# Top-k attention with a highway layer on one core: one exponential for a pair of items, and GpSimd in the search for the 32nd score

## Chip, core and metric

The kernel runs on one NeuronCore of a Trainium2 chip. The metric is device time in microseconds of one execution; before the change the median of three runs is 806.49 us (806.15 to 808.53).

## What is computed

Attention over 8 batches and 8 heads with 576 rows of 64 columns, in which each row of scores keeps its 32 largest, followed by a highway layer of 512 columns. Inputs q, k and v are normal draws times 0.1.

```python
scores = scale * np.matmul(q, k.transpose(0, 1, 3, 2))
kth = np.partition(scores, -top_k, axis=-1)[..., -top_k:-top_k + 1]   # top_k = 32
scores = np.where(scores >= kth, scores, -1000000000.0)
scores = scores - np.max(scores, axis=-1, keepdims=True)
attn = np.exp(scores)
attn = attn / (np.sum(attn, axis=-1, keepdims=True) + 1e-09)
x = np.matmul(attn, v)            # heads side by side: 4608 rows of 512
H = np.maximum(x @ w_h, 0.0)
T = 1.0 / (1.0 + np.exp(-(x @ w_t + b_t)))
out = T * H + (1.0 - T) * x
```

## The kernel before, in words

**Items and pairs.** An item is a tile of 128 score rows by 576 columns. For each batch and each of four full query tiles (`qt` 0 to 3) there is one item per head; the last 64 rows of two heads together form one "remainder" item. That makes 36 items and 18 pairs a batch (16 of full tiles, 2 of remainders), 144 pairs in all (`NG`). `step(i)` (L775) is called once per pair, and its order is written out by hand; each engine works through its own instructions in the order in which the calls issue them. One call holds parts of several pairs: masks of pair i, segment maxima of pair i+1, scores of pair i+2, masking of pair i-1, and the attention output of pair i-3.

**The search for the 32nd score** of a row goes so.
- `scores` (L296) puts both items' scores into one of two PSUM buffers (`xps`); TensorE may start on pair i+2 when pair i's buffer has had its last reader, the second `below`.
- `copy_scores` (L346) copies both items' scores from PSUM to SBUF in one ScalarE instruction of 1152 columns (`sc`).
- `segments` (L351) takes the 8 largest of each of six segments of 96 columns, 12 instructions a pair on VectorE.
- `refine` (L358) makes from them, in a handful of small VectorE instructions (`high`, `low`, `neg`, L373 to L382), the row's maximum (column `TOP` of `wall`) and a threshold (`THR`), which is surely among the 24th to 32nd score.
- `mask_count` (L395) on ScalarE marks the scores at or above the threshold and counts them by the accumulator (`csum`). `mask_add` (L407) adds that mark on TensorE to the scores in PSUM, so that `below` (L419) on VectorE finds the eight largest scores under the threshold.
- The threshold and these eight are nine candidates. `hits` (L423, VectorE) writes a 1 where the count says that the candidate is the 32nd; `pick_a` (L434, GpSimd) multiplies these flags by the candidates; `pick_b` (L438, VectorE) sums, which gives the 32nd score (`KTH`, `kth(u)`).

**What is made of it.** `biases` (L390) on GpSimd prepares for a pair the two biases of its exponentials (minus scale times each item's maximum) and of the Relu of the pair before it (`be`, one instruction of four columns; it is made to wait for the second masking of that step by `after`, L474, and `above_one` of GpSimd stands behind it). `expo` (L414) on ScalarE computes the exponential of one item, 576 columns, with its own bias: in a step the first item's stands before the copy of the next pair's scores and the second's behind it, behind the scores of pair i+2 (L819, L836). The masking of the pair follows one step later: item 0 by a Relu on ScalarE that is large from the 32nd on (`above`, L441) and a minimum on VectorE (`keep_min`, L447); item 1 by a comparison on GpSimd (`above_one`, L452) and a product on VectorE (`keep_mul`, L457), or, where GpSimd has other work, by one longer VectorE instruction (`keep`, L462).

**The rest.** A DMA transposes each masked item (L481); three steps later `values` (L487) multiplies it by V. V carries an extra column of ones (L138), so that the sum of the weights comes out beside the output. `xs_copy` (L507) takes four heads' outputs from PSUM to SBUF on ScalarE; after the eighth head of a tile, `back_xs` (L755) hands the block of 128 rows to `ffn_pieces` (L549), which divides by the sums (L557: sum plus 1e-9, times 2) and runs the highway layer in pieces: elementwise parts on GpSimd (`do_work`, L683), matmuls on TensorE, Relu and Tanh on ScalarE. `spare` (L274) issues filler matmuls that write to the same PSUM tile as the outputs, so they wait for `xs_copy` where that has the tile.

**The end.** `finish` (L943) does the last two pairs and blocks in an order of its own. Three checks (`sure`, L932, ScalarE, each a Sign with an accumulated count) test that the search was sound in all rows; only if one fails does the program compute everything again by a slow way (L1048 on).

Of the kernel before, what the change touches and what calls it, by code (L numbers as in the profile page):

```python
# [26 lines left out]
def kernel(  # L27
# [10 lines left out]
    nc = tc.nc  # L38
# [36 lines left out]
    epool = ctx.enter_context(tc.tile_pool(name="e", bufs=4))  # L75
# [35 lines left out]
    csum = consts.tile([P, NU], FP32)  # L111
    nc.vector.memset(wall[:, 0:2, KTH : KTH + 1], 0.0)
# [23 lines left out]
    for i in range(2):  # L136
        vb = consts.tile([P, H, nck, DE], BF16, name=f"vb{i}")
        nc.gpsimd.memset(vb[:, :, :, D:DE], 1.0)  # L138
        vbs.append(vb)
# [206 lines left out]
    def copy_scores(both):  # L346
        sc = scpool.tile([P, 2, S], FP32, name="sc")
        nc.scalar.copy(sc[:], both)  # L348
        return [sc[:, s, :] for s in range(2)]
# [39 lines left out]

    def biases(g):  # L390
        return nc.gpsimd.tensor_tensor(be[:, g], wall[:, 2 * g : 2 * g + 2, TOP : KTH + 1 : KTH - TOP], fac[:], ALU.mult)  # L391
# [21 lines left out]

    def expo(u, sc):  # L414
        e = epool.tile([P, S], BF16, name="e")
        nc.scalar.activation(e[:], sc, AF.Exp, bias=tb(u), scale=scale)  # L416
        return e
# [5 lines left out]
    def hits(pair):  # L423
        u0, u1 = pair[0], pair[1] + 1
        hit = cpool.tile([P, 2, NPK], FP32, name="hit")
        nc.vector.tensor_tensor(  # L426
            hit[:],
            pidx[:].unsqueeze(1).to_broadcast([P, 2, NPK]),
            csum[:, u0:u1].unsqueeze(2).to_broadcast([P, 2, NPK]),
            ALU.is_equal,  # L430
        )
# [9 lines left out]
    def above(u, sc):  # L441
        r = epool.tile([P, S], BF16, name="r")
# [9 lines left out]
    def above_one(u, sc):  # L452
        r = epool.tile([P, S], BF16, name="ro")
# [8 lines left out]
    def keep(u, sc, e):  # L462
# [6 lines left out]
            in1=e[:],  # L469
# [79 lines left out]
    def ffn_pieces(b, qt, xs):  # L549
# [4 lines left out]
        def norm():  # L554
            xs3 = xs[:, 0 : nh * DE].rearrange("p (h e) -> p h e", e=DE)
            rinv = cpool.tile([P, H], FP32, name="rinv")
            nc.vector.tensor_scalar(rinv[:, 0:nh], xs3[:, :, D], 1e-9, 2.0, ALU.add, ALU.mult)  # L557
# [82 lines left out]
    def blk_norm(k):  # L640
# [4 lines left out]
        nc.vector.tensor_scalar(rinv[:, 0:nh], xs3[:, :, D], 1e-9, 2.0, ALU.add, ALU.mult)  # L645
# [77 lines left out]
    def start_scores(g):  # L723
# [4 lines left out]
        st[g] = dict(ps=scores(pairs[g], preps[b]), sc=[None, None], et=[None, None], e=[None, None])  # L728
# [26 lines left out]
    def back_xs(g):  # L755
# [8 lines left out]
        if units[pairs[g][1]][2][-1] == H - 1:  # L764
            norms.append(ffn_pieces(b, qt, xs_t[b, qt]))

    late = []
    kind = [False]

# [5 lines left out]
    def step(i):  # L775
# [42 lines left out]
        if live:  # L818
            st[i]["e"] = [expo(pr[0], st[i]["sc"][0])]  # L819
# [15 lines left out]
        if live:  # L835
            st[i]["e"].append(expo(pr[1], st[i]["sc"][1]))  # L836
# [89 lines left out]
    cnt = consts.tile([P, 3], FP32)  # L926
    edge = consts.tile([P, 3], FP32)
    for j, e in enumerate((-(2.0**-60), 2.0**26, -(2.0**-100))):
# [14 lines left out]
    def finish():  # L943
# [7 lines left out]
        def xs_of(qt, h0, n):  # L951
# [4 lines left out]
            return dict(b=B - 1, qt=qt, xs=xs_t[B - 1, qt])  # L956
# [182 lines left out]
```

## Time and profile before

| what | value |
|---|---|
| median of three runs | 806.49 us (806.15 to 808.53) |
| the profiled run | 806.17 us |
| its span, first to last instruction | 804.5 us |
| granted TensorE clock | 0.996 of full |
| pairs, pairs of full tiles | 144, 128 |
| from the first `high` (12.49 us) to the last (780.33 us) | 767.84 us, 143 steps, 5.37 us on the mean |

All details come from the one profiled run; its time stands 1.67 us above its span. A timeline row gives the start in the span, the duration, the engine, the line of the kernel, the operation, what it writes and reads, and in brackets the idle time before it with the instruction that ended it. Durations on one engine overlap by some hundredths of a microsecond, because the next instruction starts while the last results are written; what an instruction holds its engine for is the distance from its start to the next start. A row of the groups gives the count, the busy time in us and the mean in ns, and then the idle time before these instructions with what ended it. DVE is VectorE, ACT ScalarE, POOL GpSimd, PE TensorE.

### The profile page before, as it was taken

To read this page: it belongs to the slowest core of one execution; us is meant where nothing else is said; L and a number is where in the kernel's file an instruction comes from. 1 tells how busy PE (TensorE), PEld (TensorE's weight loads), DVE (VectorE), ACT (ScalarE), POOL (GpSimd) and SP (SyncE) were. 2 spreads that over 40 slices of the span, in tenths; PEclk is the share of its full clock that TensorE was granted. 3 is DMA by queue.
4 is the path that set the end of the run, shared out by engine and by line. 5 is a ranking of instruction groups with operands and counts; after the bars stand their busy time and mean duration, and the time that the engine had idled before them with its cause. 6 is when DMAs were issued, how large, how long until landed. Compare 5 with 4: busy or idle time off the path is not lost.

```text
span 804.5 us, 20583 instructions
## 1 busy us (share of the span) xinstructions
PE 686.7 (85%) x6369; PEld 494.7 (61%) x6459; DVE 772.8 (96%) x4020; ACT 757.2 (94%) x1401; POOL 559.9 (70%) x712
## 2 busy tenths in 40 slices
PE   7889998888888888888987889888888888988884
PEld 5666766566666666566665666666666566665662
DVE  5999999999999999999999999999999999999996
ACT  5999999999999999999999999999999999999984
POOL 2666867777777767777767776777776777766750
PEclk9999999999999999999999999999999999999998
DMA  6789968996799667998669766898767996555653
GB/s 121 87 137 159 134 116 140 141 143 93 140 152 148 108 96 137 154 131 125 102 135 159 125 113 107 150 156 126 112 121 136 160 124 109 90 106 110 108 90 88
DMA packets 346359, 100.37 MB, mean 125 GB/s; under 512 B 330624, under 2 KB 338432, under 8 KB 346240
## 3 DMA queue, kind: packets, MB, share of 16 engines
q1 hardware_dynamic: 291024, 79.16, 54.1%
q0 software_dynamic: 53536, 19.34, 22.6%
q8 instruction: 53, 0.87, 0.4%
q10 hardware_dynamic: 1680, 0.46, 0.3%
q14 instruction: 66, 0.54, 0.2%
HBM read 31.72 MB, written 9.44 MB: 51 GB/s over the span
## 4 chain that ended last, share of the span: by engine, by line
ACT 37%; DVE 32%; PE 23%; DMA 4%; issue 3%; SPq 1%; another core or an unknown queue 0%; DVEq 0%; ACTq 0%
ACT m L397 15%; DVE wall L420 12%; DVE cand L353 9%; ACT e L416 7%; ACT sc L348 6%; PE pso L278 5%; ACT r L443 4%; PE xs L309 4%; PE xs L326 3%; DVE ep L450 3%; DMA xT<-xb 3%; PE fp L522 3%; PE xs L410 3%; PE pso L494 2%; ACT xs L508 2%
## 5 line engine op out<-in xcount | busy, mean ns | idle before, releaser
L353 DVE MAX8 cand<-xs 128x8 f32<-128x96 f32 x1728 | 297.5, 248 | 11.4 <-PE xs L335 6.2
L278 PE MATMUL pso<-cst,ident_b 128*128 128x252 bf16 x1841 | 246.8, 272 | 42.8 <-ACT xs L508 40.4
L454 POOL TENSOR_SCALAR ro<-sc,wall 128x576 bf16<-128x576 f32 x135 | 232.8, 1724 | 0.0
L416 ACT ACTIVATE e<-sc,be 128x576 bf16<-128x576 f32 x288 | 226.5, 787 | 0.1
L278 PEld LDWEIGHTS <-ident_b 128*128 128x128 bf16 x1841 | 173.4, 98 | 81.4 <-issue 49.5
L420 DVE MAX8 wall<-xs 128x8 f32<-128x576 f32 x288 | 204.3, 751 | 5.6 <-PE xs L410 3.5
L309 PE MATMUL xs<-kT,qT 64*128 64x256 f32 x1024 | 145.3, 400 | 30.6 <-DVE high L366 26.2
L348 ACT COPY sc<-xs 128x1152 f32<-128x1152 f32 x144 | 161.0, 1118 | 0.7 <-DVE cand L353 0.6
L309 PEld LDWEIGHTS xs<-kT,qT 64*128 64x128 f32 x1024 | 93.0, 186 | 61.3 <-issue 37.6
L397 ACT ACTIVATE m<-xs,wall 128x576 int8<-128x576 f32 x144 | 107.4, 746 | 18.2 <-DVE wall L382 17.1
L436 POOL TENSOR_TENSOR hit<-hit,wall 128x18 f32<-128x18 f32 x143 | 32.4, 227 | 121.2 <-DVE hit L426 114.0
L397 ACT ACTIVATE m<-sc,wall 128x576 int8<-128x576 f32 x144 | 111.4, 773 | 0.0
L443 ACT ACTIVATE r<-sc,be 128x576 bf16<-128x576 f32 x143 | 109.9, 769 | 0.0
L410 PE MATMUL xs<-m,ident_b 128*128 128x512 bf16 (+1 forms) x512 | 92.7, 274 | 17.3 <-ACT m L397 15.2
L494 PEld LDWEIGHTS <-et 128*128 128x128 bf16 (+1 forms) x1600 | 68.6, 100 | 19.2 <-issue 3.5
L391 POOL TENSOR_TENSOR be<-wall,fac 128x4 f32<-128x4 f32 x144 | 29.2, 203 | 72.5 <-DVE ep L460 53.7
L410 PEld LDWEIGHTS <-ident_b 128*128 128x128 bf16 x576 | 51.7, 97 | 44.8 <-issue 24.1
L494 PE MATMUL pso<-vb,et 128*128 128x65 bf16 (+1 forms) x1600 | 74.4, 194 | 4.2 <-DMA et<-ep 0.3
L450 DVE TENSOR_TENSOR ep<-e,r 128x576 bf16<-128x576 bf16 x143 | 64.6, 452 | 0.2 <-ACT r L443 0.2
L318 PEld LDWEIGHTS xs<-kd,qT 128*128 128x128 f32 x256 | 38.1, 188 | 42.5 <-issue 42.1
L318 PE MATMUL xs<-kd,qT 128*128 128x128 f32 x256 | 62.5, 326 | 0.0
L460 DVE TENSOR_TENSOR ep<-e,ro 128x576 bf16<-128x576 bf16 x135 | 60.7, 449 | 0.0
(127 smaller groups left out, 1028.9 us busy)
## 6 DMA issues: line engine op xcount, KB each, us to landing
kin<-in_k_dram SPq DMA_DIRECT2D x64, 128.0 KB, 2.9
qin<-in_q_dram SPq DMA_DIRECT2D x62, 128.0 KB, 3.1
out_dram<-s SPq DMA_DIRECT2D x30, 256.0 KB, 2.8
s<-h POOLq DMA_DIRECT2D x29, 256.0 KB, 4.0
et<-ep SPq DMA_TRANSPOSE x286, 3.3
xb<-x POOLq DMA_DIRECT2D x30, 128.0 KB, 3.0
vb<-in_v_dram POOLq DMA_DIRECT2D x28, 128.0 KB, 4.8
vb<-in_v_dram POOLq DMA_DIRECT2D x24, 64.0 KB, 3.1
```

Of the source, the lines that this page charges most:

```text
L278: nc.tensor.matmul(po["t"][:, 4 * DE : BANK], ident_b[:], cst[:, 0 : BANK - 4 * DE], start=True, stop=True, skip_group_check=True,)
L309: nc.tensor.matmul(ps[:, mo + n0 : mo + n0 + 256], qT[r : r + D, hp, qs : qs + P], kT[r : r + D, hp, n0 : n0 + 256], start=(n0 == 0), stop ...
L318: nc.tensor.matmul(ends, qT[:, hp, qs : qs + P], kd[:, hp, :], start=True, stop=True)
L348: nc.scalar.copy(sc[:], both)
L353: nc.vector.max(cand[:, s, :], sc[:, s * SEG : (s + 1) * SEG])
L397: nc.scalar.activation(m1[:].bitcast(I8)[:, 1 : 2 * S : 2], ps, AF.Sign, bias=wall[:, u, THR : THR + 1], scale=ABOVE, accum_out=csum[:, u ...
L410: nc.tensor.matmul(ps[:, s0:s1], ident_b[:], m1[:, s0:s1], start=False, stop=True, skip_group_check=True)
L416: nc.scalar.activation(e[:], sc, AF.Exp, bias=tb(u), scale=scale)
L420: nc.vector.max(wall[:, u, THR + 1 : KTH], ps)
L443: nc.scalar.activation(r[:], sc, AF.Relu, bias=eb(u), scale=BIGK)
L454: nc.gpsimd.tensor_scalar(r[:], sc, kth(u), None, ALU.is_ge)
L494: nc.tensor.matmul(pso[r0 : r0 + ql, col : col + DE], ets[s][:, c, gi * P2 : gi * P2 + ql], vb[:, h, vc, :], start=(c == 0), stop=(c == nc ...
```

## The change

For the 128 pairs of full tiles:
- One exponential covers both items (1152 columns, read from the pair's copy in SBUF), with one bias: minus scale times the larger of the two maxima. It stands where the first item's exponential stood. The two items of a remainder pair still have an exponential each, now one behind the other at that place.
- The item with the smaller maximum thus gets weights that are too small by a common factor, which the division takes out again. Only the 1e-9 of the reference has to be scaled by that factor: `distances` works out, once per block, scale times each head's maximum plus the pair's bias (one VectorE instruction for eight heads) and its exponential (one ScalarE instruction of 8 columns), and `denominators` adds 2e-9 times it to the sums in place of the instruction at L557. V's extra column is 2 instead of 1, which takes over the factor 2.
- `biases` becomes two GpSimd instructions: one column for the Relu, one for the exponential. `after` ties the one returned, the exponential's, to the masking; the other has no such tie.
- A fourth check at the end tests that no distance is below -40.

For all pairs `hits` becomes two instructions of nine columns (one per item) on GpSimd, ahead of `pick_a` there; in `finish` they run on VectorE. The buffers are regrouped (two pairs of exponentials instead of four single ones).

```diff
-        nc.gpsimd.memset(vb[:, :, :, D:DE], 1.0)
+        nc.gpsimd.memset(vb[:, :, :, D:DE], 2.0)
...
+    def joint(g):
+        return units[pairs[g][0]][1] < nfull
+
     def biases(g):
+        if joint(g):
+            top = wall[:, 2 * g : 2 * g + 2, TOP]
+            nc.gpsimd.tensor_scalar(be[:, g, 0, 1:2], wall[:, 2 * g, KTH : KTH + 1], -BIGK * (1.0 - 2.0**-24), None, ALU.mult)
+            return nc.gpsimd.tensor_scalar(be[:, g, 0, 0:1], top[:, 0:1], top[:, 1:2], -scale, ALU.max, ALU.mult)
         return nc.gpsimd.tensor_tensor(be[:, g], wall[:, 2 * g : 2 * g + 2, TOP : KTH + 1 : KTH - TOP], fac[:], ALU.mult)
...
+    def expo_both(g, both):
+        e = epool.tile([P, 2, S], BF16, name="e")
+        nc.scalar.activation(e[:], both, AF.Exp, bias=be[:, g, 0, 0:1], scale=scale)
+        return [e[:, s, :] for s in range(2)]
...
+    def distances(g):
+        u0, u1 = pairs[g][0] + 2 - H, pairs[g][0] + 2
+        nc.vector.scalar_tensor_tensor(
+            out=dist[:, u0:u1].rearrange("p (g s) -> p g s", s=2),
+            in0=wall[:, u0:u1, TOP].rearrange("p (g s) -> p g s", s=2),
+            scalar=scale,
+            in1=be[:, g + 1 - NP : g + 1, 0, 0].unsqueeze(2).to_broadcast([P, NP, 2]),
+            op0=ALU.mult,
+            op1=ALU.add,
+        )
+        low = cpool.tile([P, H], FP32, name="share")
+        nc.scalar.activation(low[:], dist[:, u0:u1], AF.Exp)
+        return low
+
+    def denominators(rinv, sums, share):
+        if share is None:
+            return nc.vector.tensor_scalar(rinv, sums, 2.0e-9, None, ALU.add)
+        return nc.vector.scalar_tensor_tensor(
+            out=rinv, in0=share[:], scalar=2.0e-9, in1=sums, op0=ALU.mult, op1=ALU.add
+        )
...
-    def hits(pair):
+    def hits(pair, eng=nc.gpsimd):
         u0, u1 = pair[0], pair[1] + 1
         hit = cpool.tile([P, 2, NPK], FP32, name="hit")
-        nc.vector.tensor_tensor(
-            hit[:],
-            pidx[:].unsqueeze(1).to_broadcast([P, 2, NPK]),
-            csum[:, u0:u1].unsqueeze(2).to_broadcast([P, 2, NPK]),
-            ALU.is_equal,
-        )
+        for s in range(2):
+            eng.tensor_scalar(hit[:, s, :], pidx[:], csum[:, u0 + s : u0 + s + 1], None, ALU.is_equal)
         return hit
...
-            nc.vector.tensor_scalar(rinv[:, 0:nh], xs3[:, :, D], 1e-9, 2.0, ALU.add, ALU.mult)
+            denominators(rinv[:, 0:nh], xs3[:, :, D], share)
...
-            norms.append(ffn_pieces(b, qt, xs_t[b, qt]))
+            norms.append(ffn_pieces(b, qt, xs_t[b, qt], distances(g) if joint(g) else None))
+
+    def exponentials(g):
+        sc = st[g]["sc"]
+        return expo_both(g, sc[2]) if joint(g) else expo_each(pairs[g], sc)
...
         if live:
-            st[i]["e"] = [expo(pr[0], st[i]["sc"][0])]
+            st[i]["e"] = exponentials(i)
         if nxt:
             copy_both(i + 1)
...
         if live:
-            st[i]["e"].append(expo(pr[1], st[i]["sc"][1]))
             pass
...
+        sure(3, dist[:], 1.0)
```

## What is forecast, before the result

> **What bounds the kernel now.** I read the shares of the page first, then the timeline of one step in the steady part, then the groups by line and form.
>
> ```profile
> span 804.5 us, 20583 instructions
> PE 686.7 (85%) x6369; PEld 494.7 (61%) x6459; DVE 772.8 (96%) x4020; ACT 757.2 (94%) x1401; POOL 559.9 (70%) x712
> ```
>
> The shares name VectorE (DVE, 96%) and ScalarE (ACT, 94%), the two engines that the change relieves. Whether that helps is decided inside a step. Here are the rows that matter around the step that begins at 420.38 (start, duration, engine, line); I count a step from one `high` (L366) to the next.
>
> ```profile
> 419.24 0.78 ACT L416 ACTIVATE e<-sc,be 128x576 bf16<-128x576 f32 x1
> ...
> 419.90 1.12 ACT L348 COPY sc<-xs 128x1152 f32<-128x1152 f32 x1
> ...
> 420.38 0.19 DVE L366 TENSOR_TENSOR high<-cand 128x48 f32<-128x48 f32 x1
> 420.48 0.20 DVE L368 TENSOR_TENSOR low<-cand 128x48 f32<-128x48 f32 x1
> ...
> 420.60 0.17 DVE L426 TENSOR_TENSOR hit<-pidx,csum 128x18 f32<-128x18 f32 x1
> 420.61 1.14 PE L309 MATMUL xs<-kT,qT 64*128 64x256 f32 x8 [0.51 <-DVE high L366]
> 420.69 0.18 DVE L370 TENSOR_SCALAR neg<-high 128x48 f32<-128x48 f32 x1
> ...
> 420.85 0.23 POOL L436 TENSOR_TENSOR hit<-hit,wall 128x18 f32<-128x18 f32 x1 [0.79 <-DVE hit L426]
> 420.90 0.80 ACT L416 ACTIVATE e<-sc,be 128x576 bf16<-128x576 f32 x1
> ...
> 421.13 0.16 DVE L439 TENSOR_REDUCE wall<-hit 128x2 f32<-128x18 f32 x1
> ...
> 421.67 0.49 PE L318 MATMUL xs<-kd,qT 128*128 128x128 f32 x2
> 421.71 0.20 DVE L382 TENSOR_REDUCE wall<-cand 128x4 f32<-128x32 f32 x1
> 421.83 0.45 DVE L460 TENSOR_TENSOR ep<-e,ro 128x576 bf16<-128x576 bf16 x1
> ...
> 421.95 0.74 ACT L397 ACTIVATE m<-xs,wall 128x576 int8<-128x576 f32 x1 [0.25 <-DVE wall L382]
> ...
> 422.20 1.91 DVE L353 MAX8 cand<-xs 128x8 f32<-128x96 f32 x11
> ```
>
> Two chains run side by side from 420.38, where the second `below` has just released a PSUM buffer. On VectorE the small operations and the two maskings follow one another until the segment maxima of the next pair (L353) start at 422.20. On TensorE the scores that those maxima read start at 420.61, their last part (L318) at 421.67, and the maxima start 0.53 us after that. **Both chains take 1.82 us.** From 422.20 to the next `high` come 1.99 us of segment maxima and 1.33 us of `below`: 5.14 us in all. Of the 142 steps between the second `high` of the kernel and the last, 65 have this floor; the rows below open the first and the last of the 65.
>
> ```profile
> 17.30 0.19 DVE L366 TENSOR_TENSOR high<-cand 128x48 f32<-128x48 f32 x1
> ...
> 763.55 0.19 DVE L366 TENSOR_TENSOR high<-cand 128x48 f32<-128x48 f32 x1
> ```
>
> The next step is of the other common kind.
>
> ```profile
> 424.25 1.25 POOL L610 TENSOR_TENSOR s<-h,x 128x512 f32<-128x512 f32 x1
> 424.57 0.38 ACT L508 COPY xs<-pso 128x260 f32<-128x260 f32 x1
> ...
> 425.00 1.02 PE L278 MATMUL pso<-cst,ident_b 128*128 128x252 bf16 x8 [0.69 <-ACT xs L508]
> ...
> 425.52 0.19 DVE L366 TENSOR_TENSOR high<-cand 128x48 f32<-128x48 f32 x1
> ...
> 425.95 1.13 PE L309 MATMUL xs<-kT,qT 64*128 64x256 f32 x8
> 426.00 0.23 POOL L436 TENSOR_TENSOR hit<-hit,wall 128x18 f32<-128x18 f32 x1 [0.50 <-DVE hit L426]
> ...
> 426.28 0.15 DVE L439 TENSOR_REDUCE wall<-hit 128x2 f32<-128x18 f32 x1
> ...
> 427.01 0.49 PE L318 MATMUL xs<-kd,qT 128*128 128x128 f32 x2
> ...
> 427.54 2.08 DVE L353 MAX8 cand<-xs 128x8 f32<-128x96 f32 x12
> ```
>
> ScalarE's copy of the outputs (L508) ends at 424.95, TensorE's eight filler matmuls (L278) wait for it, and the scores behind them start 0.43 us after `high` instead of 0.23. The maxima start 2.02 us after `high` and again 0.53 after L318. TensorE sets the end in 27 steps of this kind; in 28 others VectorE is late by itself (a block's reciprocals, the 0.8 us masking of L465, a port wait); most of the other 22 are the remainder pairs, whose scores are longer.
>
> **The change, part by part.**
>
> *One exponential for two.* The exponential at 419.24 leaves the engine after 0.66 us, the copy with twice the columns after 1.00 (419.90 to 420.90). A joint exponential should take the copy's 1.00 to 1.15, against 2 x 0.66: 0.2 us less on ScalarE in each of 128 pairs, 25 us, less 32 small exponentials of the distances at about 0.2 each, 6 us: some 19 us in all. Almost all of it is hidden. After its exponentials ScalarE goes on to the masks (L397), and those wait for VectorE's threshold (L382), by 0.25 us at 421.95:
>
> ```profile
> L454 POOL TENSOR_SCALAR ro<-sc,wall 128x576 bf16<-128x576 f32 x135 | 232.8, 1724 | 0.0
> ...
> L397 ACT ACTIVATE m<-xs,wall 128x576 int8<-128x576 f32 x144 | 107.4, 746 | 18.2 <-DVE wall L382 17.1
> ...
> L611 POOL TENSOR_TENSOR h<-h,x 128x512 f32<-128x512 f32 x30 | 37.9, 1264 | 0.1
> ...
> L436 POOL TENSOR_TENSOR hit<-hit,wall 128x18 f32<-128x18 f32 x143 | 32.4, 227 | 121.2 <-DVE hit L426 114.0 <-DVE neg L370 6.5 <-DMA et<-ep 0.7
> ...
> L611 POOL TENSOR_TENSOR h<-h,x 128x256 f32<-128x256 f32 x7 | 5.1, 727 | 0.6
> ```
>
> In 95 of the 142 steps the masks start as soon as the threshold lets them. Time that ScalarE saves there becomes more of the 17.1 us of waiting in L397's row. The chain that delays L508 (masks, Relu, an evacuation, L508) starts behind that same threshold and holds no exponential. In the 47 others ScalarE is late, but only in 16 is the next `below` late too, by 0.06 to 0.2 us, 1.7 us in all; I credit **-1.6 us**. The scores' copy moves back by 0.45 us behind the longer exponential; its first readers are the masks behind it on ScalarE, which come no later.
>
> *The flags off VectorE.* L426 holds VectorE for 0.09 us (420.60 to 420.69). In the 65 floor steps TensorE's chain still takes 1.82 us: nothing gained. In the 27 steps behind L508 the threshold, and so the whole chain, comes 0.09 earlier; in the 28 VectorE steps up to 0.09. The flags now run on GpSimd (POOL) just ahead of `high`, and there they meet its port:
>
> ```profile
> 79.99 1.26 POOL L610 TENSOR_TENSOR s<-h,x 128x512 f32<-128x512 f32 x1
> ...
> 80.72 0.60 DVE L366 TENSOR_TENSOR high<-cand 128x48 f32<-128x48 f32 x1
> ...
> 782.68 0.71 POOL L391 TENSOR_TENSOR be<-wall,fac 128x4 f32<-128x4 f32 x1 [1.64 <-DVE ep L465]
> ```
>
> `high`, 0.19 us elsewhere, took 0.60 because GpSimd's addition ran until 81.25, and a `be` of 0.2 took 0.71 beside L465. **This is the row that speaks against the change.** The Trainium skill, "SBUF — State Buffer", section "Who interferes with whom", says that a VectorE instruction with two SBUF inputs contends with a GpSimd instruction that reads SBUF, and whichever is first holds the port for its whole length. By that sentence two flag instructions and the product would cost VectorE up to 0.6 us a step, 30 us in the 55 steps that are to gain. In the row, though, `high` was done 0.07 after GpSimd's record ended (81.32 against 81.25), and it takes 0.19: the last 0.12 of the record no longer held it, so that an instruction of 0.2 holds little. Bounds for the meetings: nothing to 0.1 us a step; I take 0.04. So (27 + 28) x (0.09 - 0.04) = **-2.8 us**.
>
> *GpSimd's own lateness.* No row shows a GpSimd TENSOR_SCALAR of nine columns. From below, L436 with 18 columns takes 0.23 and a constant's memset less. From above: L611's two forms give 2.1 ns a column, so 576 columns of that kind would take 1.40, L454 takes 1.72, and if all of the 0.32 is fixed cost a flag instruction takes 0.53. I take 0.2, by the nearest row in size. At 425.50 GpSimd ends its addition. Two flags follow (2 x 0.18, they overlap a little), about 0.08 until the product may read them, the product's 0.23 and 0.06 to L439: 426.23, against 426.28 in the row above. So the flags fit, because today GpSimd idles there for VectorE's `hit` (114.0 us, the first reason in L436's row). Only where its work ends later than 0.03 us after `high` (14 steps) is the pick later than today: **+0.8 us**. The second bias instruction is free where it can: the first (the 32nd's) is bound only to L439 and has the time until L460 to run. With the distances on VectorE (32, beside the floor's new 0.09 of room) and an occasional meeting of that first bias with L460 I charge **+0.2 us**.
>
> *The tail.*
>
> ```profile
> 790.08 0.81 ACT L934 ACTIVATE signs<-wall,edge 128x288 bf16<-128x288 f32 x1
> ...
> 790.89 0.57 ACT L659 CAST xT<-xs 128x512 bf16<-128x512 f32 x1
> ```
>
> A fourth check of this size stands ahead of the turn of the last full block on ScalarE, in which nothing is idle: one slot, 790.08 to 790.89, less a little room behind it: **+0.7 us**.
>
> Sum: -1.6 - 2.8 + 0.8 + 0.2 + 0.7 = **-2.7 us**. It is made against the profiled run, 806.17 us (1.67 outside the span); the median of the runs shown is 806.49, 0.3 higher, so the forecast is 806.49 - 2.7 = **803.8 us**.
>
> **The rivals.**
>
> *Slower: the flags are dear.* One place, L436 to L439, and one price. With 0.53 us a flag, the pick is ready 2 x 0.51 + 0.08 + 0.23 + 0.06 = 1.39 us after GpSimd's other work, today 0.76 after `high`; every step whose work ends less than 0.63 ahead of `high` is late. Added up over the steps, that is 22 us in the floor steps and 14 in the others beyond their present slack: about 842. It decides from about 0.3 a flag (+4 us, all gains gone) and gives 815 at 0.4. For it: L454's dear columns. Against: both small forms of GpSimd in the trace take 0.2. The Trainium skill, "GPSIMD Engine Reference", section "3.1 Elementwise — side-by-side cycle accounting", gives a tight loop about 1.8 cycles a column; by that page L454 would be half fixed cost, 0.86 us a flag and an estimate of 920 us. No run here shows that.
>
> *Even: port meetings eat the gain.* If each step loses the upper 0.1 us to the port, the 55 steps gain nothing, and with 0.25 a flag +2 us come on top: 806 to 809. For it: the 0.60 us row; against: small instructions let go early.
>
> *Faster than forecast: the floor is not TensorE's.* Should VectorE's chain alone have set the 65 steps, they gain 0.09 each, 5.9 us more: 798. Against: 0.53 us after L318 in both kinds of step.
>
> *The change does not do what it says:* if the fourth check failed, everything would be computed again and the time would multiply. Inputs of 0.1 keep a pair's maxima close: under 1 in 100.
>
> **How the numbers follow.** About 0.3% (2.4 us) is what a measurement of this kernel can tell from no change. Forecast's case 0.48 (two thirds of it beyond 0.3%: 0.32 faster, 0.16 same). Even 0.21 (0.11 same, 0.10 slower). Dear flags 0.25, slower. Floor gives way 0.06, faster. Faster 0.38, same 0.27, slower 0.35. The likeliest case by itself reaches from 800 to 806. The range takes in the floor's case below and the dear flags up to some 0.45 us: 798 to 826, with 0.05 left out below and 0.13 above.
>
> **What would show it.** Right: the flag instructions at about 0.2 us; the product starting before `low` ends; L439 about 0.67 after `high`; the floor steps still at 5.14 with L353 0.53 after L318; ScalarE's wait for L382 grown from 17 us to 30 or more; one exponential of 1.15 to 1.3 us. Wrong: L439 later than 0.76 after `high` in most steps with waits for GpSimd (the dear flags); `high`, `low` or `neg` at 0.25 us or more on the mean (the port); floor steps under 5.1 (the floor was VectorE's).

## The result, and the profile after

| | before | after |
|---|---|---|
| median of four runs | 807.51 us (806.15 to 809.87) | 840.30 us (839.49 to 841.54) |
| ratio to before, 95% interval | | 1.0404 (1.0373 to 1.0435) |
| the profiled run, its span | 806.17, 804.5 us | 839.49, 837.4 us |
| first `high` to last, 143 steps | 767.84 us | 800.61 us |
| last `high` to the end of the span | 24.2 us | 24.9 us |

The change makes the kernel 4.0% slower. Forecast were 803.8 us and a range up to 826, so the sign is wrong and the time lies outside the range. Of the 32.9 us by which the span grew, 32.8 lie between the first `high` and the last: the steps became longer, 5.60 us on the mean instead of 5.37.

First the shares of the page, and the shares of the chain of work that ended last:

```profile
span 837.4 us, 20968 instructions
PE 708.9 (85%) x6461; PEld 499.2 (60%) x6461; DVE 781.7 (93%) x3911; ACT 740.8 (88%) x1307; POOL 712.0 (85%) x1127
...
POOL 38%; DVE 29%; PE 14%; ACT 10%; issue 6%; DMA 2%; SPq 0%; POOLq 0%; DVEq 0%; ACTq 0%
```

The chain before was this:

```profile
ACT 37%; DVE 32%; PE 23%; DMA 4%; issue 3%; SPq 1%; another core or an unknown queue 0%; DVEq 0%; ACTq 0%
```

ScalarE was relieved as intended (94% to 88%), and its part of the chain fell from 37% to 10%. GpSimd, which did not occur in the old chain at all, holds 38% of the new one. It is busy 85%, less than VectorE: the shares alone would not have named it. TensorE's granted clock was 0.986 of full in this run and 0.996 before. On the 14% of the chain that TensorE holds, that is an estimate of about 1 us, and the run with the flags first, below, is slower still at 0.998.

The groups by line and form of after, for the instructions that the change touches (count, busy us, mean ns, then the idle time before them and what ended it):

```profile
L426 ACT ACTIVATE e<-sc,be 128x1152 bf16<-128x1152 f32 x128 | 160.5, 1254 | 0.1
...
L407 ACT ACTIVATE m<-xs,wall 128x576 int8<-128x576 f32 x144 | 107.3, 745 | 64.4 <-DVE wall L384 63.9
...
L471 POOL TENSOR_SCALAR hit<-pidx,csum 128x9 f32<-128x9 f32 x286 | 95.0, 348 | 1.0 <-ACT m L407 1.0
...
L399 POOL TENSOR_SCALAR be<-wall 128x1 f32<-128x1 f32 x128 | 43.5, 340 | 15.0 <-DVE cand L380 4.8 <-DVE wall L479 1.2
L368 DVE TENSOR_TENSOR high<-cand 128x48 f32<-128x48 f32 x144 | 39.2, 272 | 0.0
L400 POOL TENSOR_SCALAR be<-wall 128x1 f32<-128x1 f32 x128 | 38.8, 303 | 30.0 <-DVE wall L384 9.5 <-DVE ep L500 6.4 <-DVE dist L438 3.9
...
L476 POOL TENSOR_TENSOR hit<-hit,wall 128x18 f32<-128x18 f32 x143 | 33.1, 232 | 26.5 <-DVE high L368 16.0 <-DVE neg L372 0.3
L479 DVE TENSOR_REDUCE wall<-hit 128x2 f32<-128x18 f32 x144 | 24.1, 168 | 21.2 <-POOL hit L476 20.1
```

Three things are to be seen. A flag instruction takes 348 ns and not 200, and the biases of one column take 340 and 303. GpSimd, which before waited 121.2 us ahead of its product, now waits 26.5 there, and VectorE waits for that product instead (20.1 us at L479; before, no wait of that kind). And ScalarE's wait for the threshold grew from 17.1 to 63.9 us: its time became waiting, more of it than the exponential saved.

The timeline shows how one step after hangs together (the step that begins at 442.60; the first and the last row are the first and the last `high` of the kernel):

```profile
11.85 0.21 DVE L368 TENSOR_TENSOR high<-cand 128x48 f32<-128x48 f32 x1
...
439.55 0.30 POOL L400 TENSOR_SCALAR be<-wall 128x1 f32<-128x1 f32 x1
439.82 1.76 POOL L494 TENSOR_SCALAR ro<-sc,wall 128x576 bf16<-128x576 f32 x1
...
441.53 1.28 POOL L650 TENSOR_TENSOR s<-h,x 128x512 f32<-128x512 f32 x1
...
442.60 0.27 DVE L368 TENSOR_TENSOR high<-cand 128x48 f32<-128x48 f32 x1
442.78 0.68 POOL L471 TENSOR_SCALAR hit<-pidx,csum 128x9 f32<-128x9 f32 x2
...
443.54 0.23 POOL L476 TENSOR_TENSOR hit<-hit,wall 128x18 f32<-128x18 f32 x1
443.80 0.17 DVE L479 TENSOR_REDUCE wall<-hit 128x2 f32<-128x18 f32 x1 [0.27 <-POOL hit L476]
...
444.05 1.00 POOL L189 DMA_DIRECT2D vb<-in_v_dram  x1 [0.28 <-issue]
444.10 0.49 PE L320 MATMUL xs<-kd,qT 128*128 128x128 f32 x2
...
444.46 0.45 DVE L500 TENSOR_TENSOR ep<-e,ro 128x576 bf16<-128x576 bf16 x1
...
444.83 2.06 DVE L355 MAX8 cand<-xs 128x8 f32<-128x96 f32 x12
445.13 0.24 POOL L399 TENSOR_SCALAR be<-wall 128x1 f32<-128x1 f32 x1
...
445.46 0.30 POOL L400 TENSOR_SCALAR be<-wall 128x1 f32<-128x1 f32 x1
445.73 1.75 POOL L494 TENSOR_SCALAR ro<-sc,wall 128x576 bf16<-128x576 f32 x1
...
812.46 0.19 DVE L368 TENSOR_TENSOR high<-cand 128x48 f32<-128x48 f32 x1
```

TensorE would let the maxima start at 444.10 + 0.53 = 444.63, and they start at 444.83: VectorE, held up by the product, is now the later of the two chains. Read on from bias to bias (L400 at 439.55, the next at 445.46). On GpSimd follow 0.27 of bias, 1.71 of comparison, 1.25 of elementwise work, 0.76 of flags with the gap behind them, 0.26 of product up to L479; then VectorE's pick, the threshold and both maskings up to 444.91 (1.11), and only behind them may the next second bias start, here 0.55 later, since GpSimd was issuing V's DMA until 445.05 and had the first bias ahead. 0.27 + 1.71 + 1.25 + 0.76 + 0.26 + 1.11 + 0.55 = 5.91. **It is a ring**: GpSimd waits for the end of VectorE's maskings and VectorE for the end of GpSimd's work, so that steps like this one take no less than the whole way round. Without anything between the masking and the bias but the usual 0.1 it is 5.46, more than the floor of 5.14. Both waits are common in this profile: VectorE waits for the product in 77 of the 142 steps, and in 87 of 128 the second bias starts within 0.2 us of the end of a masking. Of the 142 steps between the second `high` and the last, 65 had maxima within 1.86 us of `high` before, and 20 have it now.

### The profile page after: what moved, and what is told of

Read it like the earlier page. It is cut to its first block, busy times and chain, and to the rows that moved or that the text cites. A ratio compares the mean times of both kernels' runs of the same rounds, so it can differ in the third digit from the quotient of the medians.

```text
span 837.4 us, 20968 instructions
## 1 busy us (share of the span) xinstructions
PE 708.9 (85%) x6461; PEld 499.2 (60%) x6461; DVE 781.7 (93%) x3911; ACT 740.8 (88%) x1307; POOL 712.0 (85%) x1127
## 4 chain that ended last, share of the span: by engine, by line
POOL 38%; DVE 29%; PE 14%; ACT 10%; issue 6%; DMA 2%; SPq 0%; POOLq 0%; DVEq 0%; ACTq 0%
POOL ro L494 14%; DVE wall L464 9%; DVE cand L355 8%; ACT m L407 5%; POOL hit L471 5%; DVE ep L490 4%; PE pso L280 3%; POOL s L650 2%; POOL h L651 2%; PE xs L328 2%; POOL be L400 2%; PE xs L311 2%; POOL hit L476 2%; POOL h L664 2%; POOL vb L189 2%
## 5 line engine op out<-in xcount | busy, mean ns | idle before, releaser
L280 PE MATMUL pso<-cst,ident_b 128*128 128x252 bf16 x1841 | 249.4, 274 | 42.5 <-ACT xs L548 40.4
L494 POOL TENSOR_SCALAR ro<-sc,wall 128x576 bf16<-128x576 f32 x135 | 236.4, 1751 | 0.0
L311 PE MATMUL xs<-kT,qT 64*128 64x256 f32 x1024 | 148.1, 406 | 31.3 <-DVE high L368 18.8
L407 ACT ACTIVATE m<-xs,wall 128x576 int8<-128x576 f32 x144 | 107.3, 745 | 64.4 <-DVE wall L384 63.9
L426 ACT ACTIVATE e<-sc,be 128x1152 bf16<-128x1152 f32 x128 | 160.5, 1254 | 0.1
L420 PE MATMUL xs<-m,ident_b 128*128 128x512 bf16 (+1 forms) x576 | 107.0, 285 | 33.5 <-ACT m L407 31.8
L471 POOL TENSOR_SCALAR hit<-pidx,csum 128x9 f32<-128x9 f32 x286 | 95.0, 348 | 1.0 <-ACT m L407 1.0
L534 PEld LDWEIGHTS <-et 128*128 128x128 bf16 (+1 forms) x1600 | 69.0, 100 | 19.7 <-issue 3.5
L400 POOL TENSOR_SCALAR be<-wall 128x1 f32<-128x1 f32 x128 | 38.8, 303 | 30.0 <-DVE wall L384 9.5
```

The source lines that it names most:

```text
L280: nc.tensor.matmul(po["t"][:, 4 * DE : BANK], ident_b[:], cst[:, 0 : BANK - 4 * DE], start=True, stop=True, skip_group_check=True,)
L311: nc.tensor.matmul(ps[:, mo + n0 : mo + n0 + 256], qT[r : r + D, hp, qs : qs + P], kT[r : r + D, hp, n0 : n0 + 256], start=(n0 == 0), stop ...
L407: nc.scalar.activation(m1[:].bitcast(I8)[:, 1 : 2 * S : 2], ps, AF.Sign, bias=wall[:, u, THR : THR + 1], scale=ABOVE, accum_out=csum[:, u ...
L420: nc.tensor.matmul(ps[:, s0:s1], ident_b[:], m1[:, s0:s1], start=False, stop=True, skip_group_check=True)
L426: nc.scalar.activation(e[:], both, AF.Exp, bias=be[:, g, 0, 0:1], scale=scale)
L471: eng.tensor_scalar(hit[:, s, :], pidx[:], csum[:, u0 + s : u0 + s + 1], None, ALU.is_equal)
```

## The experiments

Each run stands beside runs of the kernel before on the same chip, to which its ratio is made. The mean step follows from the last column, which holds 143 of them.

| run | us | before, us | ratio (95%) | first `high` to last, us |
|---|---|---|---|---|
| flags back on VectorE | 816.93 | 808.05 | 1.0102 (1.0085 to 1.0119) | 777.90 |
| flags alone | 815.95 | 808.05 | 1.0091 (1.0072 to 1.0109) | 778.63 |
| one bias | 817.72 | 808.05 | 1.0120 (1.0098 to 1.0141) | 778.78 |
| joint exponential alone | 811.26 | 808.05 | 1.0036 (1.0024 to 1.0049) | 772.75 |
| no flags at all | 804.40 | 807.16 | 0.9967 (0.9949 to 0.9984) | 766.48 |
| flags first | 849.49 | 807.16 | 1.0532 (1.0514 to 1.0550) | 808.41 |
| both biases tied | 858.64 | 807.99 | 1.0631 (1.0614 to 1.0647) | 819.63 |
| joint exponential without distances | 807.97 | 807.16 | 1.0015 (1.0004 to 1.0026) | 769.89 |
| one more on GpSimd | 852.51 | 807.16 | 1.0557 (1.0539 to 1.0574) | 817.16 |
| ScalarE in the long steps | 809.66 | 807.99 | 1.0026 (1.0015 to 1.0037) | 772.38 |
| ScalarE from three pieces on | 807.20 | 807.99 | 0.9986 (0.9975 to 0.9997) | 768.01 |
| flags, ScalarE every third | 856.32 | 807.99 | 1.0613 (1.0586 to 1.0640) | 817.53 |
| the same, pieces paced | 835.11 | 808.70 | 1.0315 (1.0287 to 1.0343) | 796.16 |
| its control, flags on VectorE | 825.90 | 808.70 | 1.0208 (1.0186 to 1.0231) | 790.17 |

### Which part costs: four kernels

**Flags back on VectorE**, everything else as after:

```diff
-        for s in range(2):
-            eng.tensor_scalar(hit[:, s, :], pidx[:], csum[:, u0 + s : u0 + s + 1], None, ALU.is_equal)
+        nc.vector.tensor_tensor(hit[:], pidx[:].unsqueeze(1).to_broadcast([P, 2, NPK]),
+            csum[:, u0:u1].unsqueeze(2).to_broadcast([P, 2, NPK]), ALU.is_equal)
```

> The changed kernel with the flags back on VectorE as one instruction (as before the change); joint exponential and two GpSimd biases stay. Theory Q (GpSimd's queue has become the bound: flags 0.65 us and biases 0.44 us more in each step, and both count): the flags' part of GpSimd's added time is gone, so most of the loss goes; the biases' 0.44 still push GpSimd's work past the start of `high` in some steps: 809 to 818 us. Theory F (the flags alone are the loss, by their place between GpSimd's work and L479): 803 to 807. Theory E (the joint exponential and its new place cost the time): 835 to 842.

**Flags alone**: the kernel before with the reverse of that edit (and the flags on VectorE in `finish`).

> The kernel before with one part of the change alone: the flags as two GpSimd instructions; exponentials and the single bias instruction as before. Theory Q: pick_b comes about 1.0 us after the end of GpSimd's work, but that work ends 0.2 us earlier than in the changed kernel, for want of the second bias: 812 to 822 us. Theory F: 835 to 842, as the changed kernel. Theory E: 803 to 810.

**One bias**: after, with the one bias instruction of before, so that the first item's maximum is the reference of the pair:

```diff
     def biases(g):
-        if joint(g):
-            top = wall[:, 2 * g : 2 * g + 2, TOP]
-            nc.gpsimd.tensor_scalar(be[:, g, 0, 1:2], ...)
-            return nc.gpsimd.tensor_scalar(be[:, g, 0, 0:1], ...)
         return nc.gpsimd.tensor_tensor(be[:, g], wall[...], fac[:], ALU.mult)
```

> The changed kernel with the single GpSimd bias instruction of before for all pairs; the joint exponential then takes the first item's maximum instead of the larger one as its reference. Flags stay on GpSimd. Theory Q: like the flags alone, 812 to 822 us. Theory F: 835 to 842, since the biases cost nothing. If the two biases were the larger part: 804 to 810.

**The joint exponential alone**: both edits, flags on VectorE and one bias; the distances and the fourth check stay.

> Both GpSimd parts undone: flags on VectorE, one bias instruction (the first item's maximum as reference), so that the joint exponential with distances, new denominators and the fourth check are what is left of the change. Theory Q and theory F: 803 to 807 us, and the masks' wait for the threshold grown from 17 to some 30 us, since ScalarE's saving is hidden. Theory E: 835 or more.

Measured were +8.9, +7.9, +9.7 and +3.2 us. The first three lie where theory Q expected them; theory F (the flags alone, 835 or more in the second and third run) and theory E (the joint exponential) do not fit. The fourth, 811.26, lies above the 803 to 807 that Q and F named; the next section says why. Taken as differences, the two biases cost 816.93 - 811.26 = 5.7 us where the flags are on VectorE, and the flags cost 817.72 - 811.26 = 6.5 us where there is one bias. Both together cost 1.0404 x 808.05 - 811.26 = 29.4 us. **The parts do not add up: 17 us of the loss belong to the meeting of the two.** That is what a slack that is used up looks like: each part alone first uses up idle time of GpSimd.

The groups by line and form show the prices apart from each other, first in the run with the flags alone (one old bias, new flags):

```profile
L427 POOL TENSOR_SCALAR hit<-pidx,csum 128x9 f32<-128x9 f32 x286 | 89.5, 325 | 1.1 <-ACT m L397 1.1
...
L391 POOL TENSOR_TENSOR be<-wall,fac 128x4 f32<-128x4 f32 x144 | 28.9, 201 | 85.6 <-DVE ep L456 67.4 <-DVE wall L382 10.4 <-DVE ep L461 6.5
```

Then in the run with the flags back on VectorE (two new biases, old flags):

```profile
L399 POOL TENSOR_SCALAR be<-wall 128x1 f32<-128x1 f32 x128 | 40.0, 312 | 14.8 <-DVE wall L483 5.8
...
L368 DVE TENSOR_TENSOR high<-cand 128x48 f32<-128x48 f32 x144 | 38.3, 266 | 0.0
L400 POOL TENSOR_SCALAR be<-wall 128x1 f32<-128x1 f32 x128 | 38.0, 297 | 31.6 <-DVE wall L384 10.4 <-DVE ep L504 6.1 <-DVE dist L438 4.9
L480 POOL TENSOR_TENSOR hit<-hit,wall 128x18 f32<-128x18 f32 x143 | 32.0, 224 | 95.1 <-DVE hit L470 89.2 <-DVE neg L372 5.1 <-DMA et<-ep 0.8
```

One TENSOR_TENSOR of four columns takes 201 ns, and the two instructions of one column that replaced it 609 together. GpSimd's waits say how much slack is left: 85.6 us ahead of the bias with the flags alone, 95.1 ahead of the product with the two biases alone, 30.0 and 26.5 with both. The two parts also cost in different ways. With the biases alone VectorE never waits for the product; there GpSimd's later work meets `high`, which takes 266 ns on the mean instead of 200. With the flags alone `high` takes 226, and VectorE waits for the product, 4.9 us in 20 steps.

### What the joint exponential is worth, and what sets the floor

**Without distances**: the kernel above without the distances and the fourth check (the 1e-9 stays unscaled):

```diff
-            norms.append(ffn_pieces(b, qt, xs_t[b, qt], distances(g) if joint(g) else None))
+            norms.append(ffn_pieces(b, qt, xs_t[b, qt], None))
...
-            share = distances(i - NP // 2) if qt < nfull else None
+            share = None
...
-        sure(3, dist[:], 1.0)
```

> The joint exponential by itself: flags on VectorE, one bias instruction (first item's maximum as reference), and the distances, their exponentials, the scaling of the 1e-9 and the fourth check left out (the sum gets 2e-9 unscaled). Theory H (ScalarE's saving of 25 us is hidden behind the threshold, and the 3 us that the joint exponential alone lost are the distances on VectorE, 0.07 us in each floor step they stand in, and the check at the end, 0.8 us): 805 to 808.5 us, within 0.4% of the kernel before. Theory E (the later copy of the scores costs): 810 to 812.

The shares of its page, and two rows of its groups by form:

```profile
PE 685.9 (85%) x6369; PEld 494.4 (61%) x6459; DVE 772.5 (96%) x4021; ACT 736.8 (91%) x1273; POOL 559.2 (69%) x713
```

```profile
L422 ACT ACTIVATE e<-sc,be 128x1152 bf16<-128x1152 f32 x128 | 160.9, 1257 | 0.1
...
L403 ACT ACTIVATE m<-xs,wall 128x576 int8<-128x576 f32 x144 | 107.1, 744 | 38.8 <-DVE wall L384 36.8
```

1.0015 (1.0004 to 1.0026): the joint exponential is worth nothing. ScalarE is busy 736.8 us against 757.2, 20.4 less, and its wait for the threshold is 36.8 us against 17.1, 19.7 more. The time was saved and all of it turned into the wait that the prediction named. This kernel also holds the later copy of the scores and the regrouped buffers, so what these cost is in the same figure. With distances and check it is 811.26: these cost the other 2.4 us, 0.7 of it between the last `high` and the end. The rest lies in the steps: in 25 of them, at the floor, the distances (159 ns on VectorE) push the maxima from 1.82 to 1.90 us after `high`.

**No flags at all**: the kernel before, with the product reading a constant that always picks the fifth candidate:

```diff
-        nc.vector.tensor_tensor(hit[:], pidx[...], csum[...], ALU.is_equal)
...
-        nc.gpsimd.tensor_tensor(hit[:], hit[:], wall[:, u0:u1, THR:KTH], ALU.mult)
+        nc.gpsimd.tensor_tensor(hit[:], onehot[:], wall[:, u0:u1, THR:KTH], ALU.mult)
```

> The kernel before with the flags left out: GpSimd multiplies the nine candidates by a constant that always picks the fifth of them, so the 32nd score is not found; nothing is added on GpSimd, and VectorE is relieved of the 0.09 us of L426. It is the most that taking the flags off VectorE can give. Theory P (65 steps have their floor on TensorE's scores as well, only the others gain): -3 to -6 us against the kernel before, floor steps still 5.14. Theory V (the floor is VectorE's alone): -11 to -13 us, floor steps 5.05.

0.9967 (0.9949 to 0.9984), 2.8 us, just short of theory P's 3 to 6; the profiled run shows 1.4 of it between the first `high` and the last. With all of the 0.09 us a step gone and nothing in its place, the kernel gains no more than that, and the 68 steps whose maxima start within 1.86 us of `high` still take 5.14. A floor of VectorE's would have given 65 x 0.09 = 5.9 us in its steps alone: it is TensorE's, as the prediction had it. 2.8 us is also about the most that moving the flags could have brought on any engine, as large as the credit of the sum.

### The ring

**Flags first**: after, with the flags ahead of the elementwise work in GpSimd's queue, so that they are ready long before the product.

```diff
+        if live:
+            hit = hits(pr)
         do_work(nc.gpsimd, ...)
...
-            hit = hits(pr)
```

> The changed kernel with the two flag instructions issued ahead of GpSimd's elementwise work of the step instead of behind it; nothing else is moved. Theory Q (what counts is GpSimd's queue as a whole: work, flags, biases in whatever order): 836 to 843 us, no different from the changed kernel. Theory L (the flags cost by their place, late between the work and the product): 812 to 822.

1.0532 (1.0514 to 1.0550), slower still, which neither theory expected. Its timeline:

```profile
441.27 0.30 POOL L400 TENSOR_SCALAR be<-wall 128x1 f32<-128x1 f32 x1 [0.49 <-DVE ep L500]
441.54 1.75 POOL L494 TENSOR_SCALAR ro<-sc,wall 128x576 bf16<-128x576 f32 x1
...
443.27 0.62 POOL L471 TENSOR_SCALAR hit<-pidx,csum 128x9 f32<-128x9 f32 x2
443.84 1.27 POOL L650 TENSOR_TENSOR s<-h,x 128x512 f32<-128x512 f32 x1
444.41 0.77 DVE L368 TENSOR_TENSOR high<-cand 128x48 f32<-128x48 f32 x1
445.08 0.22 POOL L476 TENSOR_TENSOR hit<-hit,wall 128x18 f32<-128x18 f32 x1
445.10 0.26 DVE L370 TENSOR_TENSOR low<-cand 128x48 f32<-128x48 f32 x1
...
446.45 0.45 DVE L500 TENSOR_TENSOR ep<-e,ro 128x576 bf16<-128x576 bf16 x1
447.00 0.30 POOL L400 TENSOR_SCALAR be<-wall 128x1 f32<-128x1 f32 x1 [0.43 <-DVE ep L500]
```

The product is no longer late. Instead the addition slid over `high`, which takes 0.77 us and ends at 445.18, 0.07 after the addition's record (445.11). The ring closes by another way: bias 0.27, comparison 1.73, flags 0.57, addition 1.27, from there through `high` to the end of the second masking 1.79, and 0.10 to the next bias, 5.73 us from 441.27 to 447.00. The median step of this run is 5.66. The group of `high` in this run, and then in the run of the joint exponential alone:

```profile
L368 DVE TENSOR_TENSOR high<-cand 128x48 f32<-128x48 f32 x144 | 77.9, 541 | 0.0
```

```profile
L368 DVE TENSOR_TENSOR high<-cand 128x48 f32<-128x48 f32 x144 | 28.8, 200 | 0.0
```

It takes 541 ns on the mean instead of 200, and over 250 in 100 of the 142 steps. The Trainium skill, "SBUF — State Buffer", section "Who interferes with whom", lets a two-input VectorE instruction wait for the whole of a GpSimd instruction that was first; for these long instructions the rows agree but for the last 0.12 us. What GpSimd executes while `high` is due costs VectorE, and in after it was the small flags that stood there and shielded it.

**Both biases tied**: after, with the first bias made to wait for the second masking as well.

```diff
-            nc.gpsimd.tensor_scalar(be[:, g, 0, 1:2], ...)
+            first = nc.gpsimd.tensor_scalar(be[:, g, 0, 1:2], ...)
+            if last is not None:
+                after(first, last)
```

> The changed kernel with both bias instructions made to wait for the second masking, instead of the exponential's alone. Theory R (a ring through both engines bounds the steps: bias, comparison, work, flags and product on GpSimd, then the sum, threshold and maskings on VectorE, and again the bias; only what stands on this ring counts, and the first bias is now partly off it): the whole 0.3 us goes on the ring, up to 0.2 a step more than today: 850 to 870 us. If the first bias already stands wholly on the ring, or harms by meeting the maskings at the port: 832 to 842.

1.0631 (1.0614 to 1.0647), 858.64 us, as theory R expected. No instruction is added, and the first bias even takes less (233 ns, 340 in after); it is moved wholly onto the ring, and the step grows by 0.13 us (819.63 - 800.61 over 143). The wait moved with it, and GpSimd's share of the chain rose. The chain's shares, and the row of the first bias in the groups by form:

```profile
POOL 44%; DVE 22%; PE 12%; ACT 8%; issue 8%; DMA 3%; SPq 1%; POOLq 0%; DVEq 0%; ACTq 0%
```

```profile
L399 POOL TENSOR_SCALAR be<-wall 128x1 f32<-128x1 f32 x128 | 29.9, 233 | 61.9 <-DVE ep L502 36.0 <-DVE dist L440 16.4 <-DVE ep L507 4.4
```

**One more on GpSimd**: after, with a third instruction of one column between the two biases.

```diff
+            nc.gpsimd.tensor_scalar(extra[:], wall[:, 2 * g, KTH : KTH + 1], -1.0, None, ALU.mult)
```

> The changed kernel with one more GpSimd instruction of one column (0.3 us, into a scratch column) in each of 128 steps, ahead of the exponential's bias. Theory Q (GpSimd bounds most steps now, so that each further 0.3 us on it lengthens them by nearly that): 865 to 880 us. If GpSimd is late only in part of the steps: 845 to 860.

The added instruction in the groups by form:

```profile
L401 POOL TENSOR_SCALAR extra<-wall 128x1 f32<-128x1 f32 x128 | 31.3, 245 | 10.7
```

1.0557 (1.0539 to 1.0574), 852.51 us, below theory Q's range and in the other one: about 0.1 us a step for an instruction of 0.25 (0.09 by the two ratios, 0.12 by the profiled runs, of which this one was its kernel's slowest). On an engine that simply is full it would cost all of its time, and off the ring nothing. It is in between: GpSimd's idle time ahead of the second bias falls from 30.0 to 9.3 us, and 10.7 now stand ahead of the added instruction, so that it runs in part where GpSimd waited before.

Two figures of each profile show how the lateness reaches VectorE. The first two columns are by how much `high` is busy longer than in the run of the joint exponential alone, and how long VectorE waits for GpSimd's product; the last is by how much the way from the first `high` to the last grew.

| run | `high` longer, us | waits for the product, us | steps longer, us |
|---|---|---|---|
| flags back on VectorE | 9.5 | 0 | 5.2 |
| one bias | 2.7 | 4.5 | 6.0 |
| after | 10.4 | 20.1 | 27.9 |
| flags first | 49.1 | 0 | 35.7 |
| both biases tied | 22.4 | 28.0 | 46.9 |
| one more on GpSimd | 20.1 | 27.5 | 44.4 |

The two together come to more than what each run lost, most of all where `high` alone is longer; that the other chain hides the rest is argued and not shown. A late product is thus only one of two ways; the other is that GpSimd's late elementwise work meets `high`.

### Is there a version that gains?

**ScalarE in the long steps**: the kernel without distances; where GpSimd has much elementwise work, item 1's masking goes to ScalarE's Relu instead of VectorE's 0.8 us instruction.

```diff
-            ps_["r"].append(above_one(pu[1], ps_["sc"][1]) if len(pool_work) < (3 if last_steps else 5) else None)
+            act = len(pool_work) >= (3 if last_steps else 5)
+            ps_["r"].append((above if act else above_one)(pu[1], ps_["sc"][1]))
```

> The joint exponential by itself (run e9: flags on VectorE, one bias instruction with the first item's maximum, distances, scaling of the 1e-9 and fourth check left out), and where GpSimd had too much other work to compare (10 steps, the 0.8 us masking on VectorE) item 1 is masked as item 0 is, by a Relu on ScalarE and a minimum. Uses the time that ScalarE has free: 10 x 0.36 us less on VectorE: 804 to 807 us.

**ScalarE from three pieces on**: the same, with `act = len(pool_work) >= 3`.

> As the run before, but item 1 is masked by ScalarE in all steps in which three or more elementwise pieces wait for GpSimd. Theory R: these are the steps in which GpSimd's work ends after `high`; taking its comparison (1.75 us) off the ring there removes the port waits as well: 802 to 806 us. If ScalarE then becomes late itself: 808 to 812.

The masks' row of the second kernel in the groups by form:

```profile
L403 ACT ACTIVATE m<-xs,wall 128x576 int8<-128x576 f32 x144 | 107.4, 746 | 31.4 <-DVE wall L384 29.0
```

1.0026 (1.0015 to 1.0037), a miss, and 0.9986 (0.9975 to 0.9997), 807.20 us and so between the ranges of its two theories. The second is 0.8 us faster than before, within the 0.3% that count as no change; its wait for the threshold is 29.0 us instead of 36.8, so that ScalarE uses 8 us of what it saved. No version here gains by the joint exponential more than can be told from nothing.

**Flags with less work on GpSimd**, in three forms: flags on GpSimd and one bias, no distances, and ScalarE instead of GpSimd's comparison in every third step.

```diff
+            act = len(pool_work) >= 3 or i % 3 == 0
...
-        do_work(nc.gpsimd, 2 * dm if prev and ps_["r"][1] is None else dm)
+        do_work(nc.gpsimd, 2 * dm if prev and act else dm)
```

> As the run before, with the flags on GpSimd again, and item 1 masked by ScalarE in every third step and wherever three or more pieces wait. Theory R: in the steps without the comparison the ring is 1.75 us shorter, so the flags cost only where two steps with it follow each other with long work: 804 to 811 us, against 816 for the flags alone. If the flags' loss does not come from the ring: 814 to 818.

The second form paces the work as before, and the third is its control with the flags on VectorE:

```diff
-        do_work(nc.gpsimd, 2 * dm if prev and act else dm)
+        do_work(nc.gpsimd, 2 * dm if prev and act and len(pool_work) >= 3 else dm)
```

> Mends the run before: there GpSimd took two elementwise pieces in each step whose comparison went to ScalarE, so that it ran ahead of its data, waited in its queue for ScalarE with the flags behind, and one block of 128 rows was left unstored. Here the pieces keep their pace; flags on GpSimd, joint exponential with one bias, distances and fourth check left out, item 1 masked by ScalarE in each third step and where three or more pieces wait. Theory R: the flags' loss (7 to 8 us with the comparison in every step) shrinks, since a ring without the 1.75 us comparison has room: at most 4 us above its control with the flags on VectorE. If the flags cost by something else than the ring: 7 us or more above the control.

> The control of the run above: the same kernel with the flags on VectorE. 806 to 812 us: ScalarE takes 0.67 us more in each third step, about what the joint exponentials had saved it.

In all three one block of 128 rows is left unstored (29 issues of the output instead of 30), in the second and third too, other than expected; their times are a little too good for that. The first took 856.32 us, a miss. In it the double number of pieces makes GpSimd wait for ScalarE, with the flags queued behind, so it tells nothing of the ring. The second and third took 835.11 and 825.90, the third 14 us above its range: the flags cost 9.2 us where theory R allowed at most 4. By the sign named before (7 us or more) this speaks against a ring through GpSimd's comparison as the only way in which the flags cost. The wait for the highway layer's Relu in the view of waits (us in total, times, longest), with the flags on GpSimd and then with them on VectorE:

```profile
POOL s L646 <- ACT h L645: 34.2, 22, 3.0
```

```profile
POOL s L650 <- ACT h L649: 35.0, 22, 3.7
```

Sorted by kind of step, theory R fits one part: in the 92 steps with GpSimd's comparison the mean is 5.41 us with the flags on GpSimd and 5.40 with them on VectorE, so with this much slack they cost nothing. The difference lies in the 50 steps without the comparison, 5.87 against 5.77. There ScalarE, with a Relu more, is late with the highway layer's Relu, GpSimd stands in its queue for it (34.2 and 35.0 us), and what is queued behind is the product alone or the flags and the product. That reading of the 50 steps is argued from the waits and was not tried by itself. The steps show 6.0 of the 9.2 us. The two profiled runs are only 7.7 us apart, since the control's was its slowest; the rest stays open.

## Why the prediction was wrong, step by step

- **"I take 0.2, by the nearest row in size" failed.** A flag takes 348 ns, about the middle between the two bounds (0.2 and 0.53). The nearest rows in size were TENSOR_TENSORs; the same operation was only in L454's row. Nine columns cost 325 (with the flags alone), one column with a scalar read from a tile 297 to 303, so nearly all of it is fixed cost of the instruction. The estimate of 0.86 us a flag that the prediction worked out from the Trainium skill, "GPSIMD Engine Reference", section "3.1 Elementwise — side-by-side cycle accounting", is too high by more than a factor of two: the 348 ns decide against it.
- **"The second bias instruction is free where it can" failed, and weighed as much.** The change turned 201 ns into two instructions of 340 and 303. In after the second bias, which GpSimd's comparison stands behind, starts 2.43 us after `high` on the mean instead of 2.08, and GpSimd's work ends 0.13 us before `high` instead of 0.35. The two biases alone cost 5.7 us where +0.2 was charged. The price of a flag was bounded from both sides; the biases, the same kind of instruction, were not priced at all.
- **"+0.8 us" for GpSimd's own lateness failed by what went into it.** It was summed from the old ends of GpSimd's work, with a pick 0.73 us behind each end and no later end. In after the pick comes 0.93 us behind the end at the least. That price in the same sum over the 142 steps of the profile before gives about 9 us in 60 steps, and with each end 0.22 us later (0.35 - 0.13) about 25 us in 89 steps. These are estimates, which leave out what the other chain hides and what `high` loses, but they come near the 7.9 us of the flags alone and the 29 of both parts. So the sum itself could have shown that the parts do not add up; its prices were wrong. The ring says the same in the length of a step: 5.46 against the floor of 5.14.
- **The rival "the flags are dear" had the place and the sign, not the size.** At 0.35 a flag its own curve gave a few us (it named +4 at 0.3 and 815 at 0.4), and the flags alone cost 7.9 us. The rest of the loss came from the biases and from their meeting with the flags, which it lacked too.
- **"Almost all of it is hidden" was right.** One exponential takes 1254 ns (1.15 to 1.3 were named), ScalarE saves 20 us, and all of it goes into the wait for the threshold. The credit of 1.6 us isn't seen.
- **The floor was right**: without any flags only 2.8 us are gained, and the floor steps stay at 5.14.
- **The tail was right**: +0.7 forecast, 0.7 measured. The distances were not: they had a part in the +0.2, and distances and check together cost 2.4 us, 0.7 of it in the tail.
- **The port was judged right for small instructions and missed for long ones.** With the flags alone `high` takes 226 ns on the mean instead of 201 and `low` 225 instead of 200, 0.05 us a step where 0.04 was charged. But in after GpSimd's work runs later and meets `high`: 272 ns on the mean, 10 us over the run. The prediction named "0.25 us or more on the mean" as a sign of being wrong; that sign came, with the first sign, L439 later than 0.76 us after `high` (L479 now stands at 1.01 on the mean).

## What to carry to other kernels

When work is moved to an engine that "waits anyway", find what its waits end with and what waits for it in turn: if the two close a ring, add up the whole ring with every instruction on it at its price and compare that with the floor of the step. If you add up late steps by the old slack instead, move the old ends by every instruction that the change adds ahead of them. Splitting a small instruction into two costs a second fixed price, so count instructions, not columns, and price each new one by a row of the same operation. And a saved microsecond is worth what stands behind the wait that it turns into: here that was nothing.

## What was not expected of the hardware

- On GpSimd a TENSOR_SCALAR whose scalar is read from a tile takes about 0.3 us even for a single column (297 to 303 ns), more than a TENSOR_TENSOR of four columns (201) or of 18 (224). With constants as scalars one column takes 233 to 245 ns (L399 tied, `extra`). In after, where L399 is not tied and can run beside VectorE's maskings, it takes up to 0.74 us and 340 ns on the mean; tied behind them it never takes more than 0.25.
- An order of GpSimd's queue that brings a result earlier can be worse than the late one, by what runs while VectorE's two-input instructions are due: 541 ns a `high` with a long addition there, 272 with the flags there, 200 with neither.
